# All twelve inner blocks of the last two batches in one run of groups, five of the pairs by Strassen's scheme

## The chip, the core and the metric

The kernel runs on one core of a Trainium2 chip. The metric is the device time of one execution in microseconds (us). The core has a matrix engine (TensorE, PE in the profile), three engines for elementwise work (VectorE as DVE, ScalarE as ACT, GpSimd as POOL) and a queue engine (SyncE, SP) from which nearly all DMAs are issued. Each engine runs its instructions in the order in which the program lists them. A difference of under 0.2% is about what a measurement of this kernel cannot tell from none.

## The reference, cut to what matters

```python
# q, k, v: (4 batches, 12 heads, 448, 64); weights are float64
scores = q @ k^T / 8, causal mask, softmax
x = softmax @ v                      # back to (4, 448, 768)
h = relu(x^T @ w_tok1) @ w_tok2      # mixes the 448 tokens through 256
u = x + h^T
out = u + relu(u @ w_ch1) @ w_ch2    # mixes the 768 channels through 1536
```

The channel mixer is the large part. Its 1536 inner channels are twelve **inner blocks** of 128. Each float32 operand is split into a high and a low part, so every product takes three matmuls: high by high, high by low, low by high.

## The kernel before, in words

**Attention** goes by pairs of heads, 24 pairs, six to a batch. `load_pair` and `prep` bring q and k in and transpose them. `heads` (L672) multiplies them (`qk`, line L695, fourteen small matmuls that the profile shows as 28 instructions). They use quarters of the array, 64 rows by 64 columns, and `QUARTERS` gives their order. The scores land in four PSUM banks, one for each entry of `ROUND`, and seven blocks follow: `low` on DVE (L712), `expo` on ACT (L724), then `guard`, `recip` and a normalisation each. Pairs 0 to 11 are turned by PE (`by_tensor`, L781). Pairs 12 to 23 are split into 16-bit halves, turned by DMA and merged (`by_dma`, L801). `values` (L882) multiplies by v, and `xturn` (L928) turns the result. The buffers `prob0` to `prob3` have two copies each. In `by_dma` a pair takes one copy for its probabilities and the other for the split halves, so the next pair's `qk` can begin only when the splits have read the first copy.

**The token mixer** (`tokens`, L974 and L1007) runs for each third of a batch and adds into `u`. `split_u` makes the high and low parts of `u`.

**The channel mixer** has two forms. `channels(stage)` (L1056) takes one quarter (three inner blocks) for the batches that `STAGES` names: 108 matmuls of 448 columns for a quarter and a batch. `group(number)` takes blocks for batches 2 and 3 together. A pair of blocks goes by Strassen's scheme: seven products of 9 matmuls (L1376) in place of 72, then the multiplication back (L1444), 72 matmuls. `mixtures` makes the sums T1 to T4 of the two batches that the scheme needs, `combined` the sums of the weights. `hidden` (L1304) applies the relu and makes high and low mid tiles, in the rings `gh` and `gl` of six. `add` (L1120) adds a result into `u`, and the last one of a batch and column block starts `store` or, at the very end, `finish` (L1457).

**The order of the work** is written by a planner. `Plan.job` records each step with its cost on the engines that may do it, its needs, the buffers it holds and a rank. `Plan.emit` (L137) steps through a modelled time: each free engine takes the ready step of lowest rank whose buffers are open. Attention of pair g has rank 2g. A plain stage has rank 27 plus 6 for each stage before it, so fills in on PE between the pairs. Evacuations and re-read weights have rank -5 or -6. In the first 75 us, when PE has nothing ready and the modelled busy share is low, `emit` puts in a filler matmul that computes nothing (`keep_warm`, L602). The real engines then follow this order, whatever the model got wrong.

Before the change `STAGES` is quarter 0 for batch 0; quarters 1, 2 and 3 for batches 0 and 1; quarter 0 for batches 1 and 2; quarter 3 for 2 and 3; quarter 0 for batch 3. `GROUPS` holds three pairs, blocks 3 to 8. The last stage runs after the groups.

Of the kernel before, what the change touches and what calls it, by code (L numbers as in the profile page):

```python
# [19 lines left out]

class Slot:


    def __init__(self, ring):
        self.ring = ring
        self.index = ring.uses
        self.left = 0
        self.tile = None
        ring.uses += 1

    def take(self):
        self.ring.taken.append(self)
# [16 lines left out]
class Bank:  # L49


    def __init__(self, plan, kind, share):
        self.plan, self.kind, self.share = plan, kind, share
        self.left = 0
        self.bank = None

# [4 lines left out]
    def take(self):  # L61
        p = self.plan
        self.bank = p.banks.pop(0)
        p.used[self.kind] = p.used.get(self.kind, 0) + 1
# [6 lines left out]
class Job:  # L71
    def __init__(self, order, costs, fn, rank, moved, lock=False):
        self.order, self.costs, self.fn, self.rank, self.moved, self.lock = order, costs, fn, rank, moved, lock
        self.waits = 0
        self.ready = 0.0
        self.after = []
        self.takes = []
        self.holds = []
        self.done = False
        self.engine = None  # L80


class Plan:
# [7 lines left out]
    WINDOW, KEEP, WARM = 3400.0, 0.65, 75000.0  # L91
    LAG = {"pe": 230.0, "act": 150.0, "dve": 150.0, "pool": 150.0, "sp": 100.0}
    OWN = {"pe": 0.0, "act": 100.0, "dve": 130.0, "pool": 100.0, "sp": 100.0}
# [28 lines left out]
    def job(self, costs, fn, needs=(), holds=(), rank=0.0, moved=0.0, lock=False):  # L122

        j = Job(len(self.jobs), costs, fn, rank, moved, lock)
        for n in needs:
            if n is not None:
                n.after.append(j)
                j.waits += 1
        for s in holds:
            if s.left == 0:  # L130
                j.takes.append(s)
            s.left += 1
            j.holds.append(s)
        self.jobs.append(j)
        return j

    def emit(self):  # L137
        now = 0.0
        free = dict.fromkeys(self.ENGINES, 0.0)
        port = {"dve": 0.0, "pool": 0.0}  # L140
        dma = 0.0

        def until(j, e, t):
# [3 lines left out]
            return t + j.costs[e]  # L147
# [17 lines left out]
        while left:  # L165
# [3 lines left out]
            for e in self.ENGINES:  # L169
# [4 lines left out]
                while ready[e]:  # L174
# [4 lines left out]
                    open_ = all(s.open() for s in j.takes) and self.fits(j)  # L179
# [29 lines left out]
                end = until(pick, e, now)  # L209
                if e == "pool" or (e == "dve" and pick.lock):  # L210
                    port[e] = end
                free[e] = end
                if e == "pe":
                    self.spans.append((now, end))
                if pick.moved:
                    dma = end = max(end + 650.0, dma) + pick.moved
                    end += 800.0
                heapq.heappush(events, (end, 0, pick.order, pick))
# [25 lines left out]
def kernel(  # L244
# [72 lines left out]
    def act_ps(n):  # L317
        return 160.0 + 0.833 * n

    def act_sb(n):  # L320
        return 200.0 + 0.833 * n

    def dve1(n):
        return 150.0 + 1.04 * n

    def dve2(n):
        return 150.0 + 0.55 * n

    def pool1(n):
        return 230.0 + 0.85 * n  # L330

    def pool2(n):
        return 270.0 + 2.1 * n

    def pe(*ns):
        return sum(max(109.0, 0.458 * n) for n in ns)

    def move(n):
        return n / 290.0
# [45 lines left out]
    def narrow(n, shape, source, f, rank, needs=(), raw=None):  # L385
# [31 lines left out]
        j = plan.job({"sp": 520.0}, load, holds=[raw], rank=rank, moved=move(shape[0] * n * 8))  # L417
        j = plan.job({"act": act_sb(n)}, size, [j, *needs], [raw, f], rank)
# [5 lines left out]
    def token_weights():  # L424
        work = [(w_tok1, w1hi, w1lo, c, 0, DT) for c in range(NCH)]
        work += [(w_tok2, w2hi, w2lo, c, o, S // 2) for c in range(NM) for o in (0, S // 2)]
        for n, (src, hi, lo, c, o, w) in enumerate(work):
# [10 lines left out]
            a = narrow(w, [P, 1, w], source, f, TRANK, raw=slot(("wh", "wl")[n % 2]))  # L438
# [17 lines left out]
    def channel_weights(stage, o):  # L456
# [5 lines left out]
        size = P * NT * P * 4  # L462
        if stage < NQT:
            def source():
# [12 lines left out]
                {"sp": 520.0},  # L477
                lambda e: nc.sync.dma_start(out=scratch[m], in_=flat(f.tile)),
                got, [f], rank, moved=move(size),
            )  # L480
        else:
            got = [plan.job(
                {"sp": 520.0},
# [3 lines left out]
                [saved[m]], [f], rank, moved=move(size),  # L487
            )]
        if stage == len(STAGES) - 1 and o < NF:

            wh, wl = slot("ws"), slot("wsl")
            p, q = homes_of(wh)

            def hi(e):
                wh.tile = home_of(wh, 0)
                copy(e, wh.tile, flat(f.tile))

            def lo(e):
                wl.tile = home_of(wh, 1)
                minus(e, wl.tile, flat(f.tile), wh.tile.bitcast(F32))  # L500

            w = NT * P
            a = plan.job({"act": act_sb(w), "pool": pool1(w)}, hi, got, [f, wh, p], rank)
            return wh, wl, a, plan.job(
                {"pool": pool2(w), "dve": dve1(w)}, lo, [a], [f, wh, wl] + list({p, q}), rank, lock=True
            )
        wh, wl = slot("wh"), slot("wl")
        a = plan.job(
            {"act": act_sb(NT * P), "pool": pool1(NT * P)},
            lambda e: copy(e, make(wh, [P, NT * P], F32R), flat(f.tile)), got, [f, wh], rank,  # L510
        )
        b = plan.job(
            {"pool": pool2(NT * P), "dve": dve1(NT * P)},
            lambda e: minus(e, make(wl, [P, NT * P], F32R), flat(f.tile), wh.tile.bitcast(F32)),
            [a], [f, wh, wl], rank, lock=True,
        )
        return wh, wl, a, b

    def reread(sources, saves, rank):
# [7 lines left out]
        return f, plan.job({"sp": 520.0}, load, saves, [f], rank, moved=move(P * NT * P * 4))  # L527
# [16 lines left out]
    def parts(f, got, rank):  # L544
# [3 lines left out]
            {"act": act_sb(NT * P), "pool": pool1(NT * P)},  # L548
            lambda e: copy(e, make(wh, [P, NT * P], F32R), flat(f.tile)), [got], [f, wh], rank,
# [15 lines left out]
    QUARTERS = ((0, 0, 6), (0, 1, 5), (1, 2, 4), (1, 3, 3), (0, 1, 1), (1, 3, 2), (1, 2, 0),  # L565
                (1, 1, 5), (1, 0, 6), (0, 3, 3), (0, 2, 4), (0, 3, 2), (0, 2, 0), (1, 1, 1))
# [59 lines left out]
    def load_pair(g):  # L626
        b, t = divmod(g, NT)
        for nm, src in (("k", k), ("q", q), ("v", v)):
# [26 lines left out]
            js = [plan.job({by: 520.0 * n}, fn, holds=[s], rank=2.0 * g + RL + (VL if nm == "v" else 0.0), moved=1274.0)]  # L655
# [16 lines left out]
    def heads(g):  # L672
# [16 lines left out]
        def qk(e):  # L689
            for r in range(len(ROUND)):  # L690
                bank(scores[r])
                kept(probs[r])
            for j, r, c in QUARTERS:
                lanes = LANES[1 - j if r in CROSS else j]
# [6 lines left out]
        holds = scores + probs + [ke, qe, stat]  # L701
        m = plan.job({"pe": 1900.0}, qk, ready + [last_qk[0]], holds, rank)
        last_qk[0] = m
        for r, cs in enumerate(ROUND):
            ps = scores[r]
            for c in cs:
# [22 lines left out]
                a = plan.job({"dve": 80.0 + dve1(wide(c))}, low, [m, start], [ps, probs[r], stat], rank)  # L729
                if start is None:  # L730
                    start = a
                exps.append(plan.job({"act": 480.0 + 0.833 * wide(c)}, expo, [a], [probs[r], stat], rank))
            for rg in RG:
                if r == rg[-1]:
# [13 lines left out]
                    rc = plan.job({"act": 230.0, "pool": 250.0, "dve": 170.0}, guard, exps, [stat], rank, lock=True)  # L748
                    rc = plan.job({"dve": 180.0}, recip, [rc], [stat], rank)
# [9 lines left out]
    def by_tensor(g, rcs, probs, stat, part, wide):  # L759
# [5 lines left out]
        for r, cs in enumerate(ROUND):  # L765
            norms = []
            for c in cs:
                def norm(e, c=c, r=r):
# [4 lines left out]
                    {"pool": pool1(w) + 90.0, "dve": dve2(w) + 60.0, "act": act_sb(w) + 95.0}, norm, [rcs[r]], [probs[r], stat], rank, lock=True  # L773
# [20 lines left out]
            a = plan.job({"pe": pe(0, 0, 0, 0)}, flip, norms + [prev, blank[f"prob{r}", probs[r].index % PB]], [ps, pt, probs[r]], rank)  # L794
# [6 lines left out]
    def by_dma(g, rcs, probs, stat, part, wide):  # L801
# [6 lines left out]
        for r, cs in enumerate(ROUND):  # L808
            both = halves[r]
            parts = [blank[f"prob{r}", probs[r].index % PB]]  # L810
            for c in cs:
                w = wide(c)

                def norm(e, c=c, r=r):
# [3 lines left out]
                    {"pool": pool1(w) + 90.0, "dve": dve2(w) + 60.0, "act": act_sb(w) + 95.0}, norm, [rcs[r]],  # L818
# [18 lines left out]
            a = plan.job({"sp": 1250.0}, turn, [a], [both, t16], rank, moved=1570.0)  # L837
# [15 lines left out]
            costs = {"act": 220.0 * n + 0.97 * 8 * P, "dve": 150.0 * n + 0.55 * 8 * P}  # L853
# [9 lines left out]
    def values(g):  # L863
# [10 lines left out]
        for part in ((0, 1), (2, 3)):  # L874
# [15 lines left out]
            cost = sum(52.0 + QC * STEPS[n][3] / 0.6 for n in part)  # L890
            prev = plan.job({"pe": cost}, pv, js + pdone + [prev], [ps, s, pt, u], rank)
# [14 lines left out]
        u_ready[b, t] = plan.job({"act": 200.0 + act_ps(S), "dve": 140.0 + dve1(S)}, evac, [prev] + first, [ps, u], rank)  # L906

    def xturn(g):
# [24 lines left out]
        a = plan.job({"pe": pe(0, 0, 0, 0)}, turn, [u_ready[b, t]], [ps, utile[b]], rank)  # L933
# [22 lines left out]
    u_split = {}  # L956
    us = {}

    def tokens(b, hf):
# [38 lines left out]
        for t in range(hf * NTH, (hf + 1) * NTH):  # L998
# [19 lines left out]
            u_split[b, t] = plan.job({"dve": dve1(S)}, plus, [a], [ps, utile[b]], WRANK)  # L1018
# [27 lines left out]
    def channels(stage):  # L1046
# [53 lines left out]
        for o in range(NF):  # L1100
            wh, wl, wa, wb = channel_weights(stage, NF + o)
            for i in range(2):
                for b in bs:
# [13 lines left out]

                    add(b, t, ps, prev, (stage, t) == (len(STAGES) - 1, NT - 1))

    def add(b, t, ps, prev, final=False):  # L1120
# [7 lines left out]
        if b == B - 1:  # L1128

            ready.append(unmixed[t])  # L1130
# [5 lines left out]
        if times + 1 == (NQT if b < 2 else 2 + len(GROUPS)):  # L1136
# [420 lines left out]
```

## Time and profile before

| | before |
|---|---|
| median of 3 runs | 565.9 us (565.84 to 566.09) |
| profiled execution, its own time | 566.33 us |
| its span, first to last instruction | 564.6 us |
| PE busy | 548.2 us (97%) |
| DVE, ACT, POOL busy | 395.0, 304.7, 223.1 us |
| granted TensorE clock | 1.0 throughout, 2.4 GHz |

A row of a group of instructions reads: line, engine, operation, written tile and read tiles, count, then busy time and mean duration of one, then idle time of the engine before them and what ended it. Matmuls are pipelined, so the duration of one is longer than the distance from one start to the next.

### The profile page before, as it was taken

To read this page: it belongs to the slowest core of one execution; us is meant where nothing else is said; L and a number is where in the kernel's file an instruction comes from. 1 tells how busy PE (TensorE), PEld (TensorE's weight loads), DVE (VectorE), ACT (ScalarE), POOL (GpSimd) and SP (SyncE) were. 2 spreads that over 40 slices of the span, in tenths; PEclk is the share of its full clock that TensorE was granted. 3 is DMA by queue.
4 is the path that set the end of the run, shared out by engine and by line. 5 is a ranking of instruction groups with operands and counts; after the bars stand their busy time and mean duration, and the time that the engine had idled before them with its cause. 6 is when DMAs were issued, how large, how long until landed. Compare 5 with 4: busy or idle time off the path is not lost.

```text
span 564.6 us, 10295 instructions
## 1 busy us (share of the span) xinstructions
PE 548.2 (97%) x3512; PEld 473.5 (84%) x3512; DVE 395.0 (70%) x925; ACT 304.7 (54%) x746; POOL 223.1 (40%) x320
## 2 busy tenths in 40 slices
PE   8789999999999999999999999999999999999996
PEld 4467888878888988988988988988999998999995
DVE  4575868588777677778867687566576668677835
ACT  3678888787687566776667754674143120111010
POOL 2465675535352321430353621353356546232001
PEclk9999999999999999999999999999999999999999
DMA  6777647576988689789996766766221030312525
GB/s 112 157 154 149 155 104 174 161 180 150 197 224 190 149 203 204 177 222 200 217 217 132 151 111 122 148 126 127 62 74 56 29 111 2 111 55 86 126 57 99
DMA packets 230340, 77.37 MB, mean 137 GB/s; under 512 B 206544, under 2 KB 219024, under 8 KB 230288
## 3 DMA queue, kind: packets, MB, share of 16 engines
q1 hardware_dynamic: 217056, 74.99, 58.6%
q10 hardware_dynamic: 13232, 1.72, 1.8%
q8 instruction: 28, 0.46, 0.3%
q14 instruction: 24, 0.20, 0.1%
HBM read 49.15 MB, written 14.94 MB: 114 GB/s over the span
## 4 chain that ended last, share of the span: by engine, by line
PE 90%; SPq 3%; ACT 3%; DMA 2%; DVE 1%; issue 0%; POOL 0%; DVEq 0%; ACTq 0%
PE ps L1056 48%; PE ps L1444 8%; PE ps L882 7%; PE ps L1376 6%; PE ps L1007 5%; PE ps L974 5%; PE ps L695 5%; PE ps L781 3%; SPq L635 2%; PE ps L928 2%; DMA wl<-in_moe_w_tok_dram 1%; ACT prob L724 1%; SPq L400 1%; ACT pt L343 0%; DMA kq<-in_q_dram 0%
## 5 line engine op out<-in xcount | busy, mean ns | idle before, releaser
L1124 DVE TENSOR_TENSOR u<-ps,u 128x448 f32<-128x448 f32 x107 | 66.3, 622 | 47.1 <-PE ps L1056 33.6
L724 ACT ACTIVATE prob<-prob,stat 128x448 f32<-128x448 f32 (+6 forms) x168 | 84.0, 504 | 26.1 <-DVE stat L712 25.9
L345 POOL TENSOR_SCALAR prob<-prob,stat 128x448 f32<-128x448 f32 (+6 forms) x125 | 69.9, 572 | 39.7 <-DVE stat L746 36.7
L1056 PE MATMUL ps<-gh,wh 128*128 128x448 f32 x216 | 80.6, 373 | 0.0
L1056 PE MATMUL ps<-gh,wl 128*128 128x448 f32 x216 | 79.0, 366 | 0.0
L1056 PE MATMUL ps<-gl,wh 128*128 128x448 f32 x216 | 79.0, 366 | 0.0
L1056 PE MATMUL ps<-uh,wh 128*128 128x448 f32 x198 | 75.0, 379 | 0.0
L1056 PE MATMUL ps<-uh,wl 128*128 128x448 f32 x198 | 72.5, 366 | 0.0
L1056 PE MATMUL ps<-ul,wh 128*128 128x448 f32 x198 | 72.4, 366 | 0.0
L345 POOL TENSOR_SCALAR wh<-wf 128x768 fp32r<-128x768 f32 x27 | 23.1, 854 | 113.4 <-PE ps L1056 65.1
L712 DVE CUSTOM_DVE_ANT_0 prob<-ps,mask 128x448 f32<-128x448 f32 (+6 forms) x168 | 62.3, 412 | 0.3 <-PE ps L695 0.3
L743 POOL TENSOR_SCALAR stat<-stat 128x3 f32<-128x3 f32 (+1 forms) x43 | 13.3, 309 | 96.5 <-ACT prob L724 95.0
L882 PE MATMUL ps<-pt,vraw 128*64 128x448 f32 (+3 forms) x384 | 46.8, 386 | 1.4 <-ACT pt L343 1.4
L882 PEld LDWEIGHTS ps<-pt,vraw 128*64 128x64 f32 x384 | 25.4, 136 | 25.0 <-issue 14.0
L349 ACT COPY pt<-pt 128x512 uint16<-128x512 uint16 (+1 forms) x46 | 36.8, 875 | 15.5 <-DMA pt<-prob 15.4
L1056 PEld LDWEIGHTS ps<-gh,wh 128*128 128x128 f32 x216 | 40.6, 188 | 3.7
L1056 PEld LDWEIGHTS ps<-gl,wh 128*128 128x128 f32 x216 | 40.6, 188 | 3.5 <-DVE gl L1092 0.3
L1056 PEld LDWEIGHTS ps<-gh,wl 128*128 128x128 f32 x216 | 40.5, 188 | 3.2
L695 PEld LDWEIGHTS ps<-kq,kq 64*64 64x64 f32 x672 | 36.0, 132 | 8.3 <-issue 4.2
L695 PE MATMUL ps<-kq,kq 64*64 64x448 f32 (+6 forms) x672 | 41.8, 383 | 0.0
L354 DVE TENSOR_TENSOR wl<-wf,wh 128x768 fp32r<-128x768 f32 x35 | 35.9, 1033 | 8.5 <-ACT wh L343 4.9
L1056 PEld LDWEIGHTS ps<-uh,wh 128*128 128x128 f32 x198 | 37.2, 188 | 3.7
(144 smaller groups left out, 1224.2 us busy)
## 6 DMA issues: line engine op xcount, KB each, us to landing
wraw<-in_moe_w_ch_dram SPq DMA_DIRECT2D x24, 768.0 KB, 5.3
wf<-scratch SPq DMA_DIRECT2D x30, 384.0 KB, 3.2
scratch<-wf SPq DMA_DIRECT2D x24, 384.0 KB, 5.8
vraw<-in_v_dram SPq DMA_DIRECT2D x48, 96.0 KB, 2.4
out_dram<-kq SPq DMA_DIRECT2D x68, 56.0 KB, 1.8
kq<-in_k_dram SPq DMA_DIRECT2D x60, 56.0 KB, 3.9
kq<-in_q_dram SPq DMA_DIRECT2D x56, 56.0 KB, 2.5
gh<-in_k_dram SPq DMA_DIRECT2D x36, 56.0 KB, 2.3
```

Source lines behind the costliest of these rows:

```text
L345: eng[e].tensor_scalar(dst, src, scale, 0.0, op0=ALU.mult, op1=ALU.add)
L349: nc.scalar.copy(out, in_)
L354: eng[e].tensor_tensor(dst, a, b, op=ALU.subtract)
L695: nc.tensor.matmul(scores[r].tile[lanes, WHERE[c]:WHERE[c] + wide(c)], lhsT=qe.tile[LANES[j], c * QC:(c + 1) * QC], rhs=ke.tile[LANES[j], ...
L712: nc.vector.tensor_tensor_reduce(out=part(c, r), in0=ps.tile[:, WHERE[c]:WHERE[c] + wide(c)], in1=mask[:, S - wide(c):], scale=-SCALE, sca ...
L724: nc.scalar.activation(part(c, r), part(c, r), AF.Exp, bias=stat.tile[:, 0, AT[c]:AT[c] + 1], scale=-1.0, accum_out=stat.tile[:, 1, AT[c]: ...
L882: nc.tensor.matmul(ps.tile[LANES[j], c * QC:(c + nq) * QC], lhsT=s.tile[:, kb, j], rhs=view[:, o:o + nq, j], start=(kb == 0), stop=(n == 3),)
L974: nc.tensor.matmul(ps.tile[:, :PART], lhsT=w[:, c, m * P:(m + 1) * P], rhs=x.tile[:, c, :], start=(n == 0), stop=(n == len(work) - 1),)
L1056: nc.tensor.matmul(ps.tile[:, :S], lhsT=x.tile[:, at_:at_ + P], rhs=y, start=(n == 0 and i == 0), stop=(n + 1 == w[2] and i == 2),)
L1124: eng[e].tensor_tensor(u, ps.tile[:, :S], u, op=ALU.add)
L1376: nc.tensor.matmul(ps.tile[:, :S], lhsT=l()[:, t * P:(t + 1) * P], rhs=r, start=(t == 0 and n == 0), stop=(t == half - 1 and n == 2),)
L1444: nc.tensor.matmul(ps.tile[:, :S], lhsT=l.tile[:, t * P:(t + 1) * P], rhs=r.tile, start=(n == 0), stop=(n == 3 * len(fs) - 1),)
```

## The change

It rewrites four things. The stages and groups are set anew, with five Strassen pairs for batches 2 and 3, block 11 alone first and block 10 joined to the last pair. A second home for mid tiles is used by every other group. `qk` becomes two steps, its matmuls in another order. The planner gets other costs, a model of the DMA rings, and a table `NUDGE` of about 130 rank shifts.

```diff
+NUDGE = {
+    "narrow.load": {3.5: -1, 16: -19, 22: -34, 23: 5, 25: -5, 26: -3, 27: -62},
+    "heads.low": {2: -26, 8: 3, 12: -4, 16: -0.2, 18: -16, 24: -9, 26: 2, 32: -1, 42: -41, 44: 11},
+    "group.product.do": {55.98: 6, 56.79: 21, 57.06: 6, 60.87: 9, 64.68: 38, 64.95: 46, 67.68: 14, 68.49: 15,
+        68.76: 37, 69.03: 17},
...
 class Plan:
-    WINDOW, KEEP, WARM = 3400.0, 0.65, 75000.0
-    LAG = {"pe": 230.0, "act": 150.0, "dve": 150.0, "pool": 150.0, "sp": 100.0}
+    LEAD, SWITCH, RING = 1400.0, 100.0, 128.0
+    SLACK, SETTLED = 1.1, 30000.0
+    WINDOW, KEEP, WARM = 3400.0, 0.7, 75000.0
+    LAG = {"pe": 200.0, "act": 145.0, "dve": 130.0, "pool": 80.0, "sp": 100.0}
...
+        name = fn.__qualname__.replace("<locals>.", "").partition(".")[2]
+        rank = rank + NUDGE.get(name, {}).get(round(rank, 3), 0.0)
...
-    STAGES = ((0, (0,)), (1, (0, 1)), (2, (0, 1)), (3, (0, 1)), (0, (1, 2)), (3, (2, 3)), (0, (3,)))
-    LAP = 0.0
-    GROUPS = ((3, 4), (5, 6), (7, 8))
+    STAGES = ((0, (0,)), (1, (0, 1)), (2, (0, 1)), (3, (0, 1)), (0, (1,)))
+    LAP = 0.1
+    FIRST_GROUP = 4.5
+    SPAN = (0.34, 0.68, 1.01)
+    GROUPS = ((11,), (0, 1), (2, 3), (4, 5), (6, 7), (8, 9, 10))
...
     def act_ps(n):
-        return 160.0 + 0.833 * n
+        return 65.0 + 0.833 * n
...
-    QUARTERS = ((0, 0, 6), (0, 1, 5), (1, 2, 4), (1, 3, 3), (0, 1, 1), (1, 3, 2), (1, 2, 0),
-                (1, 1, 5), (1, 0, 6), (0, 3, 3), (0, 2, 4), (0, 3, 2), (0, 2, 0), (1, 1, 1))
+    QUARTERS = ((0, 0, 6), (1, 0, 6), (0, 1, 5), (1, 1, 5), (0, 1, 1), (1, 1, 1),
+                (0, 3, 3), (1, 3, 3), (0, 2, 4), (1, 2, 4), (0, 3, 2), (1, 3, 2), (0, 2, 0), (1, 2, 0))
...
-        holds = scores + probs + [ke, qe, stat]
-        m = plan.job({"pe": 1900.0}, qk, ready + [last_qk[0]], holds, rank)
-        last_qk[0] = m
+        made = {}
+        for rg, cost in zip(RG, (930.0, 740.0)):
+            holds = [x for r in rg for x in (scores[r], probs[r])] + [ke, qe, stat]
+            m = plan.job({"pe": cost}, lambda e, rg=rg: qk(e, rg), ready + [last_qk[0]], holds, rank, tiled=True)
+            last_qk[0] = m
+            made.update(dict.fromkeys(rg, m))
...
-                a = plan.job({"dve": 80.0 + dve1(wide(c))}, low, [m, start], [ps, probs[r], stat], rank)
+                a = plan.job({"dve": 82.0 + 0.975 * wide(c)}, low, [m, start], [ps, probs[r], stat], rank)
...
-                exps.append(plan.job({"act": 480.0 + 0.833 * wide(c)}, expo, [a], [probs[r], stat], rank))
+                exps.append(plan.job({"act": 277.0 + 0.857 * wide(c)}, expo, [a], [probs[r], stat], rank))
...
-            at = 7.89 if stage == len(STAGES) - 1 else stage
-            return CRANK + CSTEP * (at + (0.5 if stage == len(STAGES) - 1 else 1.0) * (count - n) / total) - CLEAD
+            return CRANK + CSTEP * (stage + len(bs) * 0.5 * (count - n) / total) - CLEAD
...
-        if b == B - 1:
-            ready.append(unmixed[t])
+        if b >= B - 2:
+            ready += unmixed[b, t]
...
-            p1, i1, e1 = again(t)
-            p2, i2, e2 = again(t + half)
-            x1, j1, f1 = mix("T1", t, p1, at(u3, t), ALU.subtract, [i1] + n3, [e1, u3])
+            v = t + half
+            n2, m2, n3, m3 = u_whole[B - 2, t], u_whole[B - 2, v], u_whole[B - 1, t], u_whole[B - 1, v]
+            x1, j1, f1 = mix("T1", t, at(u2, t), at(u3, t), ALU.subtract, [n2, n3], [u2, u3])
...
+    def second_home():
+        if not second:
+            second.append(slot("u"))
+        x = second[0]
+        g = {n: [plan.slot("g2", 3), plan.slot("g3", 3), [x]] for n in ("11", "22", "12")}
...
+        g["21"] = [slot("h1h"), slot("h1l"), []]
+        return g
...
-            g = {n: (slot("gh"), slot("gl")) for n in names}
+            g = second_home() if number % 2 else {n: (slot("gh"), slot("gl"), []) for n in names}
...
-    for stage in range(len(STAGES) - 2):
+    mixtures()
+    for stage in range(len(STAGES)):
         channels(stage)
-    mixtures()
-    channels(len(STAGES) - 2)
-    for number in range(len(GROUPS)):
-        group(number, 6.0 + number * 0.63)
-    channels(len(STAGES) - 1)
+    at = FIRST_GROUP
+    for number, fs in enumerate(GROUPS):
+        group(number, at)
+        at += SPAN[len(fs) - 1]
```

`again`, which rebuilt batch 2's `u` from its parts, is gone, since no plain stage adds into batches 2 and 3 any more. Homes of the mixtures now include the token weights, dead by then. The wide copies of re-read weights may go to ACT alone, no longer to POOL. `add` finishes both batches at the last column block of the last group.

## Rows read from the trace of the kernel before

**Rows 1.** The page's first part: busy time, share of the span, instructions.

```profile
PE 548.2 (97%) x3512; PEld 473.5 (84%) x3512; DVE 395.0 (70%) x925; ACT 304.7 (54%) x746; POOL 223.1 (40%) x320
```

**Rows 2.** Busy time by stage: stretch, length, engines, clock, DMA share, GB/s.

```profile
7.00:60.00 53.00, 44.78 (x415) 32.60 (x418) 34.43 (x134) 39.61 (x129) 26.33 (x55) 1.00 0.72 144
60.00:127.00 67.00, 65.96 (x567) 56.40 (x561) 47.85 (x148) 55.99 (x169) 38.15 (x60) 1.00 0.62 158
...
163.00:372.00 209.00, 209.00 (x1337) 181.47 (x1336) 154.56 (x380) 137.80 (x302) 64.80 (x96) 1.00 0.80 175
372.00:403.60 31.60, 31.60 (x176) 28.41 (x174) 20.23 (x33) 14.67 (x31) 12.63 (x15) 1.00 0.56 116
...
453.00:536.00 83.00, 81.60 (x401) 74.82 (x400) 60.50 (x90) 11.83 (x19) 27.36 (x23) 1.00 0.29 83
536.00:560.00 24.00, 23.53 (x115) 21.15 (x114) 12.29 (x20) 2.49 (x4) 3.52 (x3) 1.00 0.40 74
560.00:565.00 5.00, 0.73 (x4) 0.37 (x4) 1.02 (x3) 0.00 (x0) 0.00 (x0) 1.00 0.47 94
```

**Rows 3.** PE's waits, 7 to 60 us (two) and 60 to 565 us (one).

```profile
PE ps L781 <- POOL prob L345: 3.6, 3, 1.5
PE ps L781 <- ACT prob L343: 1.9, 1, 1.9
...
PE ps L1444 <- DVE gl L1312: 1.4, 1, 1.4
```

**Rows 4.** Fillers: their group in 7 to 60 us; one run of twelve.

```profile
L602 PE MATMUL ps<-mask 128*128 128x512 bf16 x39 | 10.2, 380 | 0.0
...
8.76 2.76 PE L602 MATMUL ps<-mask 128*128 128x512 bf16 x12
```

**Rows 5.** The chain that ended last, 400 to 470 us: start, us, what.

```profile
403.76 49.45 PE ps L1056 x243
453.21 10.96 PE ps L1376 x54
...
465.46 2.06 DVE gl L1312
```

**Rows 6.** Line L1056 alone, up to the last token matmul and behind it.

```profile
0.00:403.60 403.60, 205.96 (x946) 173.54 (x946) 1.00 0.74 163
403.60:453.10 49.50, 49.50 (x243) 45.44 (x242) 1.00 0.18 50
```

**Rows 7.** The same chain: nine matmuls after whole-array work, and after a qk.

```profile
139.11 1.83 PE ps L1056 x9
...
195.39 1.66 PE ps L695 x14
197.06 2.04 PE ps L1056 x9
```

**Rows 8.** Timeline of pair 0: low on DVE, expo on ACT, blocks of 448 and 384.

```profile
9.64 0.59 DVE L712 CUSTOM_DVE_ANT_0 prob<-ps,mask 128x448 f32<-128x448 f32 x1
...
10.16 0.55 DVE L712 CUSTOM_DVE_ANT_0 prob<-ps,mask 128x384 f32<-128x384 f32 x1
...
10.28 0.67 ACT L724 ACTIVATE prob<-prob,stat 128x448 f32<-128x448 f32 x1 [6.20 <-DVE stat L712]
...
10.94 0.60 ACT L724 ACTIVATE prob<-prob,stat 128x384 f32<-128x384 f32 x1
```

**Rows 9.** Timeline of PE: first and last qk turned by DMA, last product with v.

```profile
126.99 1.74 PE L695 MATMUL ps<-kq,kq 64*64 64x448 f32 x28
...
363.03 1.74 PE L695 MATMUL ps<-kq,kq 64*64 64x448 f32 x28
...
388.79 1.95 PE L882 MATMUL ps<-pt,vraw 128*64 128x448 f32 x16
```

**Rows 10.** DVE by group, 403.6 to 453 us: adds, and differences of the mixtures.

```profile
L1124 DVE TENSOR_TENSOR u<-ps,u 128x448 f32<-128x448 f32 x14 | 8.7, 624 | 8.1 <-PE ps L1056 7.6
L1184 DVE TENSOR_TENSOR kq<-kq,kq 128x448 f32<-128x448 f32 x6 | 6.1, 1023 | 0.0
...
L1184 DVE TENSOR_TENSOR kq<-kq,u 128x448 f32<-128x448 f32 x3 | 1.9, 628 | 0.0
```

More of the change, by code (lines that the diff above doesn't have):

```diff
@@ L131, in job @@
                 j.takes.append(s)
+            elif s not in j.takes:
+                j.joins.append(s)
             s.left += 1
@@ L146, in until @@
                 t = max(t, port["dve" if e == "pool" else "pool"])
-            return t + j.costs[e]
+            return t + j.costs[e] * (self.SLACK if now >= self.SETTLED and e not in ("pe", "sp") else 1.0)
         ready = {e: [] for e in self.ENGINES}
@@ L178, in emit @@
                         continue
-                    open_ = all(s.open() for s in j.takes) and self.fits(j)
+                    open_ = all(s.got for s in j.joins) and all(s.open() for s in j.takes) and self.fits(j)
                     if open_ and len(j.costs) > 1:
@@ L486, in channel_weights @@
                 ),
-                [saved[m]], [f], rank, moved=move(size),
+                [saved[m]], [f], rank, moved=1200.0,
             )]
[L489 to L517, printed above, removed]
+        return parts(f, got, rank, stage >= NQT)
     def reread(sources, saves, rank):
@@ L835, in turn @@
                 nc.sync.dma_start_transpose(out=t16.tile[:, r], in_=both.tile.bitcast(U16))
-            a = plan.job({"sp": 1250.0}, turn, [a], [both, t16], rank, moved=1570.0)
+            a = plan.job({"sp": 1310.0}, turn, [a], [both, t16], rank, moved=1900.0, ring=73)
             def merge(e, r=r):
@@ L1116, in channels @@
                     )
[L1118 removed]
+                    add(b, t, ps, prev)
     def add(b, t, ps, prev, final=False):
@@ L1332, in place @@
             count += n
-            if len(fs) == 1:
-                return CRANK + CSTEP * (at + span * (count - n) / total) - CLEAD
             done = count - n
-            return CRANK + CSTEP * (at + (0.005 * done - LAP if done < 63 else 0.005 * done)) - CLEAD
+            return CRANK + CSTEP * (at + (0.005 * done - LAP if len(fs) > 1 and done < 63 else 0.005 * done)) - CLEAD
         gs = {b: [] for b in bs}
-        if len(fs) == 1:
-            wh, wl, wa, wb = parts(*up_block(fs[0], rank), rank)
+        split_block = parts if len(fs) == 1 else spared
@@ new lines, in group, with product, do, first @@
+        if len(fs) > 1:
+            ws = combined(*fs[:2], rank)
+            def product(wname, bname):
+                wh, wl, wd, wslots = ws[wname]
+                rows = [mixed[bname, t] for t in range(half)]
+                ps = share("w")
+                def do(e):
+                    bank(ps)
+                    for t in range(half):
+                        hi, lo = rows[t][0](), rows[t][1]()
+                        for n, (l, r) in enumerate(((wh, hi), (wh, lo), (wl, hi))):
+                            nc.tensor.matmul(
+                                ps.tile[:, :S], lhsT=l()[:, t * P:(t + 1) * P], rhs=r,
+                                start=(t == 0 and n == 0), stop=(t == half - 1 and n == 2),
+                            )
+                return ps, plan.job(
+                    {"pe": pe(*[S] * 9)}, do, wd + [j for r in rows for j in r[2]],
+                    [ps] + wslots + [z for r in rows for z in r[3]], place(9),
+                )
+            names = ("11", "22", "12", "21")
+            g = second_home() if number % 2 else {n: (slot("gh"), slot("gl"), []) for n in names}
+            def first(p):
+                f, (ps, j) = slot("kq"), p
+                def do(e):
+                    nc.scalar.copy(make(f, [P, S], F32), ps.tile[:, :S])
+                return f, plan.job({"act": act_ps(S)}, do, [j], [ps, f], WRANK - 1)
+            def plus(a, p, to=None, needs=()):
+                (src, ja), (ps, j) = a, p
+                f = to or slot("kq")
+                def do(e):
+                    if to is None:
+                        make(f, [P, S], F32)
+                    nc.vector.tensor_tensor(f.tile, src.tile, ps.tile[:, :S], op=ALU.add)
+                return f, plan.job(
+                    {"dve": dve1(S)}, do, [ja, j, *needs], [ps] + list({src, f}), WRANK - 1
+                )
+            def out_of(name, c):
+                f, j = c
+                return hidden(None, lambda: f.tile, *g[name][:2], [j], [f] + g[name][2])
+            p1 = product("A11", "B11")
+            c1 = first(p1)
+            p2 = product("A12", "B21")
+            p6 = product("S2", "T2")
+            p5 = product("S1", "T1")
+            p7 = product("S3", "T3")
+            p3 = product("S4", "B22")
+            p4 = product("A22", "T4")
+            u2 = plus(c1, p6)
+            r11 = out_of("11", plus(c1, p2, c1[0], [u2[1]]))
+            u4 = plus(u2, p5)
+            u3 = plus(u2, p7, u2[0], [u4[1]])
+            c22 = plus(u3, p5)
+            r22 = out_of("22", c22)
+            r12 = out_of("12", plus(u4, p3, u4[0]))
+            r21 = out_of("21", plus(u3, p4, u3[0], [c22[1]]))
+            gs[B - 1] = [r11, r21]
+            gs[B - 2] = [r12, r22]
@@ L1434, in group @@
-        downs = [parts(*down_block(f, rank), rank) for f in fs]
+        downs = [(split_block if n == 2 else parts)(*down_block(f, rank), rank) for n, f in enumerate(fs)]
         for t in range(NT):
```

304 lines of the change are left out of this document (164 added, 140 removed).

## The prediction

> **What bounds the kernel now.** I read the page's first part first: PE is busy for 97% of the span, and the next engine, DVE, for 70% [rows 1]. So time goes only with PE work, or with PE time that does no work. Busy time by stage shows where that second kind lies [rows 2]. From 60 us to the end PE is never idle for long: 1.0 us missing up to 127 us, nothing up to 453, 1.4 us in the groups, 0.5 behind them, 4.3 in the tail. In 7 to 60 us it is busy for 44.8 of 53 us, so 8.2 are idle. Part of what counts as busy there is filler: 39 filler matmuls, at 2.76 us for a run of twelve 0.23 each, 9.0 us [rows 4]. The head thus loses 17.2 us. PE's longest waits in it are for normalised tiles from POOL and ACT, 3.6 and 1.9 us [rows 3]: pairs of heads are not ready in time. The one wait of size later on is 1.4 us for a mid tile's low part [rows 3], at the border from products to the multiplication back. The chain that ended last shows the price of PE work: 243 matmuls in 49.45 us, 0.2035 us each [rows 5].
>
> **Part 1, fewer matmuls.** Plain quarters: before, 1+2+2+2+2+2+1 = 12 of 108 matmuls, 1296; three pairs at 63+72 add 405, in all 1701. After: 1+2+2+2+1 = 8 quarters, 864; block 11 alone 72; four pairs 540; the last group 63+36+108 = 207; in all 1683. Eighteen matmuls at 0.2035 us are **-3.7 us**, all on the path. Longer accumulations spare some adds on DVE, which is off the path; the two more pairs add sums and combined weights there, and DVE has 21 of 83 us spare in the group stage [rows 2].
>
> **Part 2, qk in two steps.** The same 28 instructions take 1.66 us in the chain; nine whole-array matmuls behind them take 2.04 us instead of 1.83 [rows 7]. So one visit to the quarter-array work costs 0.21 us, in and out together. Where other work comes between the halves there is a second visit. No row shows a half by itself: the ends are 0 (halves always adjacent) and 24 x 0.21 = 5.0 us. For pairs 0 to 11 I take them as adjacent. For the twelve turned by DMA the second half waits for the splits of its own two buffers, so other work comes between: 12 x 0.21 = **+2.5 us**.
> The Trainium skill, "TensorEngine Tiling (Array Packing)", Key Properties, says that a change of the tiling mode, not of the tile alone, drains the engine; it speaks against this part of the change. The 0.21 us in the row agrees with it.
>
> **Part 3, the second home.** Every other pair writes its mid tiles elsewhere, and `LAP` moves its products ahead of the last multiplications back, so PE has work while the low parts are made. The 1.4 us of [rows 3] go, between 0 and -1.4 for each border shown; I take **-1.4 us**. Next late would be the weights of the next pair, whose first matrix waits for two products of the pair before.
>
> **Part 4, the head.** Nothing is removed there, but pairs start differently. The planner booked 0.695 us for a `low` of 448 columns and 0.853 for its `expo`. The starts of the next blocks show 0.52 and 0.66 [rows 8]. The new formulas give 0.519 and 0.661. So the old plan held each pair for about 0.17 us a block too long on either engine, seven blocks a pair: 1.2 and 1.3, together 2.5 us, and put fillers and other work where the pair was in truth ready. The halved `qk` also lets `low` of the first two banks be planned before the last two are written, about 0.7 us of the 1.66. Six pairs begin in 7 to 60 us. The ends are 0, if DVE and ACT, busy for 34 and 40 of the 53 us, hand the waits on to each other, and -17.2, if all that is lost comes back. I take a third, **-6 us**, 1 us a pair: nearer to 0, because ACT is the busier engine there and its work stays. The changed costs and rank shifts can also lose here; that is inside the ends of the last rival.
>
> **Part 5, the cover behind attention.** This part can turn the sign. Before the last token matmul at 403.6 us PE ran 946 plain matmuls, and 243 more behind it [rows 6], while the sums for Strassen were made. After the change only 864 plain ones exist, plus about 30 of block 11 that need nothing of batch 3's last third. So PE has 52 fewer, 10.6 us, to put between the pairs, less the 2.5 us of part 2: its fill ends 8.1 us before the old place of that matmul, whatever the head gives to both. The twelve pairs turned by DMA start 21.5 us apart (126.99 to 363.03, eleven steps) and the last one's product with v starts at 388.79 [rows 9]. If the step shrinks by 0.7 us, 12 x 0.7 = 8.4 us, the tokens are in time. I expect more: 2.5 us of too-long booking per pair, and a first half that no longer waits for all four splits. PE is at 100% there and DVE at 154.6 of 209 us, ACT at 137.8 [rows 2], so there is room. Behind the last token matmul about two thirds of the sums, eight differences of 0.63 to 1.02 us, and twelve adds of 0.62 remain for DVE [rows 10]: some 7 + 7.5 us, with 3 us for low parts 17.5. PE's cover is the rest of block 11 and two products without sums, about 60 matmuls or 12.2 us. Five us are short unless batch 1's last quarter (22 us of PE) is still there, which it is when the pairs speed up. The ends are 0 and +13 (8 + 5); I take **+1 us**.
>
> DMAs: re-read weights stay at 30, loads, transposes and stores keep their count; SP's queue is moved past nothing new but the stores of batch 1. These must end before the second home, batch 1's old residual, comes free. Tail: two batches instead of one finish, but one inside the other's last 1.8 us of matmuls; 0, at most +0.5 us beside the 4.3.
>
> **Sum.** -3.7 + 2.5 - 1.4 - 6 + 1 = -7.6 us on the profiled execution's 566.3 us (span 564.6 and 1.7 around it): 558.7. That execution lies 0.4 above the median of 565.9, so **558.3 us**.
>
> **Rivals.**
> *The head comes back almost whole.* Thirteen of 17.2 us instead of 6: 551. For it: the fillers stand where the model, not the chip, said that nothing was ready. Against: ACT's 40 of 53 us.
> *PE runs dry behind attention* (slower). If the pairs' step does not shrink, the last token matmul stands 8 us behind the end of the fill, and the sums add 5: +13 in place of +1, 570.3. It decides where the step stays above 20.8 us. For it: PE was full there before only because stages of batches 2 and 3 could be put in. Against: booked costs that were too long, and DVE with a quarter of its time free.
> *Every half drains the array.* Part 2 at its upper end, +2.5 more, and the extra visits take the head's 6 us: 566.8, no change. The row gives the price of a visit, but not how often halves part.
> *The second home does nothing.* It is batch 1's residual buffer. If its stores come late, the first pair's low parts wait there and each of five borders keeps its 1.4 us: 7 us in place of 0, 565.3.
>
> **How the numbers follow.** Forecast 0.60, head 0.16, dry 0.13, drained array 0.07, no second home 0.04. The forecast's own range is 552 to 565 from the ends of parts 2 and 4. The low end, 549, takes in the first rival with some room. The upper end, 568, takes in the third and fourth and leaves most of the dry case out. A difference under 0.2% (1.1 us) is about what a measurement of this kernel can't tell from none. Faster by more: the forecast, the first rival and the odd part of the fourth, 0.79. Same: third and part of the fourth, 0.08. Slower: 0.13.
>
> **What would show it.** Right: 1683 matmuls on the three lines; fewer than 39 fillers and less than 8.2 us idle in 7 to 60 us; the pairs' step under 20.8 us; the last token matmul before 390 us; no PE wait of over 1 us at a border of groups. Wrong: a PE wait of several us for a mixture or a mid tile right behind the last token matmul, or a head as long as before.

## The result, and the profile after

The changed kernel takes **558.9 us** (median of 4, 557.7 to 560.3) against 566.0 for the one before in the same runs: ratio **0.987, 95% interval 0.985 to 0.990**. 558.3 was forecast. The profiled execution took 557.66 us with a span of 555.5 and a granted clock of 1.0.

The page's first part, and the stages of the kernel after (columns as in [rows 2]):

```profile
PE 547.3 (99%) x3492; PEld 462.8 (83%) x3492; DVE 413.9 (75%) x964; ACT 338.7 (61%) x820; POOL 159.9 (29%) x247
```

```profile
7.00:60.00 53.00, 50.69 (x470) 35.31 (x470) 38.79 (x154) 47.33 (x162) 26.94 (x59) 1.00 0.71 145
...
127.00:357.00 230.00, 230.00 (x1504) 195.76 (x1505) 177.64 (x420) 176.23 (x396) 75.19 (x99) 1.00 0.81 180
357.00:535.00 178.00, 178.00 (x863) 161.57 (x862) 134.21 (x212) 51.91 (x81) 16.58 (x13) 1.00 0.31 78
535.00:555.50 20.50, 16.72 (x85) 14.83 (x83) 10.64 (x19) 1.31 (x4) 0.00 (x0) 1.00 0.68 121
```

PE's missing time is now almost all in the head and the tail: 2.3 of 53 us idle in 7 to 60 us, where [rows 2] had 8.2; 0.7 from 60 to 127 us; nothing from 127 to 535 us; 3.8 in the tail. PE's waits in the head, and the only one behind it (in place of [rows 3]), then the fillers (in place of the first of [rows 4]):

```profile
PE ps L737 <- DVE kq L707: 1.4, 1, 1.4
PE ps L737 <- DVE stat L791: 0.9, 1, 0.9
...
PE ps L927 <- ACT pt L410: 0.5, 1, 0.5
```

```profile
L641 PE MATMUL ps<-mask 128*128 128x512 bf16 x34 | 9.2, 380 | 0.0
```

The 3.6 and 1.9 us waits for normalised tiles are gone, and so is the 1.4 us at the border of the groups. The plain channel line, up to the last token matmul and behind it ([rows 6]), and the timeline of PE at the first and last pair turned by DMA and the last product with v ([rows 9]):

```profile
0.00:357.00 357.00, 160.82 (x747) 137.80 (x747) 1.00 0.77 171
357.00:410.00 53.00, 24.32 (x117) 21.89 (x117) 1.00 0.59 127
```

```profile
113.46 1.75 PE L737 MATMUL ps<-kq,kq 64*64 64x448 f32 x28
...
310.10 1.09 PE L737 MATMUL ps<-kq,kq 64*64 64x448 f32 x12
311.13 1.95 PE L927 MATMUL ps<-pt,vraw 128*64 128x448 f32 x16
313.01 0.81 PE L737 MATMUL ps<-kq,kq 64*64 64x256 f32 x10
...
342.35 1.95 PE L927 MATMUL ps<-pt,vraw 128*64 128x448 f32 x16
```

The pairs' step is (310.10 - 113.46) / 11 = 17.9 us, from 21.5. The last token matmul stands 46 us earlier, and 117 plain matmuls still lie behind it. Of the channel lines there are 864 plain, 72 up-products of the two single blocks (11 and 10, 36 each), 315 products and 432 multiplications back: 1683, as forecast.

**Where the time went.** The trace was split at each PE start, the time up to the next start given to the instruction before it. The span fell by 9.1 us: idle time from 15.0 to 7.0 us (-8.0), fillers from 14.7 to 13.5 (-1.2), channel matmuls from 353.3 to 348.9 (-4.4), qk from 40.4 to 43.2 (+2.8), the turns of the probabilities by PE from 21.4 to 22.4 (+1.0), the rest +0.7. Idle and fillers together are called **PE's lost time** below: 29.7 us before, 20.5 after, of it in 7 to 60 us 17.2 and 10.1.

### The profile page after: what moved, and what is told of

Its sections match the earlier page's. It is cut to its first block, busy times and chain, and to the rows that moved or that the text cites. A ratio compares the mean times of both kernels' runs of the same rounds, so it can differ in the third digit from the quotient of the medians.

```text
span 555.5 us, 10290 instructions
## 1 busy us (share of the span) xinstructions
PE 547.3 (99%) x3492; PEld 462.8 (83%) x3492; DVE 413.9 (75%) x964; ACT 338.7 (61%) x820; POOL 159.9 (29%) x247
## 4 chain that ended last, share of the span: by engine, by line
PE 92%; ACT 3%; DMA 2%; SPq 1%; issue 1%; DVE 1%; POOL 0%; ACTq 0%; DVEq 0%; POOLq 0%
PE ps L1104 31%; PE ps L1523 16%; PE ps L1432 12%; PE ps L927 8%; PE ps L737 6%; PE ps L1021 5%; PE ps L1054 4%; PE ps L826 3%; PE ps L1503 3%; PE ps L641 2%; PE ps L973 2%; DMA wraw<-in_moe_w_ch_dram 1%; SPq L674 1%; ACT prob L769 1%; ACT pt L410 0%
## 5 line engine op out<-in xcount | busy, mean ns | idle before, releaser
L1104 PE MATMUL ps<-uh,wh 128*128 128x448 f32 x144 | 54.4, 378 | 0.0
L1104 PE MATMUL ps<-gh,wh 128*128 128x448 f32 x144 | 53.4, 370 | 0.0
L1104 PE MATMUL ps<-gl,wh 128*128 128x448 f32 x144 | 52.7, 366 | 0.0
L1104 PE MATMUL ps<-gh,wl 128*128 128x448 f32 x144 | 52.7, 366 | 0.0
L1104 PE MATMUL ps<-uh,wl 128*128 128x448 f32 x144 | 52.7, 366 | 0.0
L1104 PE MATMUL ps<-ul,wh 128*128 128x448 f32 x144 | 52.6, 366 | 0.0
L410 ACT ACTIVATE wh<-wf 128x768 fp32r<-128x768 f32 x21 | 17.3, 844 | 52.5 <-PE ps L1523 37.9
L737 PE MATMUL ps<-kq,kq 64*64 64x64 f32 (+6 forms) x672 | 45.8, 387 | 2.3 <-DVE kq L707 1.4
L769 ACT ACTIVATION_READ_ACCUMULATOR prob<-prob,stat 128x1 f32 x168 | 32.9, 196 | 0.0
L410 ACT ACTIVATE prob<-prob,stat 128x256 f32<-128x256 f32 (+5 forms) x65 | 27.7, 462 | 6.6 <-DVE stat L791 6.4
```

The costliest lines, as they stand in the source:

```text
L410: nc.scalar.activation(dst, src, AF.Copy, scale=scale)
L737: nc.tensor.matmul(scores[r].tile[lanes, WHERE[c]:WHERE[c] + wide(c)], lhsT=qe.tile[LANES[j], c * QC:(c + 1) * QC], rhs=ke.tile[LANES[j], ...
L769: nc.scalar.activation(part(c, r), part(c, r), AF.Exp, bias=stat.tile[:, 0, AT[c]:AT[c] + 1], scale=-1.0, accum_out=stat.tile[:, 1, AT[c]: ...
L1104: nc.tensor.matmul(ps.tile[:, :S], lhsT=x.tile[:, at_:at_ + P], rhs=y, start=(n == 0 and i == 0), stop=(n + 1 == w[2] and i == 2),)
```

## The experiments

All ratios are to the kernel before. PE's lost time and qk's time are counted as above, in one profiled execution of each kernel; a "visit" is a run of qk matmuls with nothing else between them.

| kernel | median us | ratio (95%) | lost time, all (7 to 60 us) | qk us, visits |
|---|---|---|---|---|
| before | 566.0 | 1 | 29.7 (17.2) | 40.4, 24 |
| after | 558.9 | 0.985 to 0.990 | 20.5 (10.1) | 43.2, 36 |
| e1 after again | 557.4 | 0.982 to 0.989 | 20.0 (10.3) | 43.2, 36 |
| e2 no shifts | 564.6 | 0.996 to 1.001 | 24.0 (11.0) | 44.1, 39 |
| e4 one home | 556.8 | 0.981 to 0.985 | 21.2 (10.4) | 43.2, 36 |
| e11 one home, no lap | 557.9 | 0.984 to 0.987 | 20.7 (10.3) | 43.3, 36 |
| e5 new plan, old structure | 569.2 | 1.004 to 1.007 | 25.1 (12.4) | 44.6, 38 |
| e8 first quarters joined | 580.2 | 1.024 to 1.027 | 37.1 (11.2) | 44.6, 38 |
| e5b one shift less | 560.7 | 0.989 to 0.992 | 20.7 (10.8) | 43.8, 38 |
| e9 same, qk whole | 566.8 | 1.001 to 1.004 | 30.3 (15.3) | 40.4, 24 |
| e10 same, halves for pairs 0 to 5 | 563.1 | 0.994 to 0.997 | 26.1 (8.9) | 42.1, 28 |
| e13 shifts of rank 24 up, and negative | 559.7 | 0.987 to 0.991 | 20.6 (10.0) | 43.5, 37 |
| e12 shifts of rank 0 to below 16 | 568.2 | 1.002 to 1.006 | 28.1 (12.9) | 43.3, 36 |
| e14 shifts of rank 24 up, qk whole | 571.7 | 1.007 to 1.011 | 32.0 (15.0) | 40.4, 24 |

### The changed kernel once more

No edit.

> The changed kernel once more, nothing edited. Median 557.5 to 560.5 us. In the trace on record its matmuls of 448 columns stand 206.7 ns apart in most of the group stage, 203 before. If that belongs to the program's order, it stands at the same places again; if it is chance of the execution, elsewhere or not at all.

Measured 557.4 us. The chain in the group stage shows what differed between the two profiled executions of one program; first the one after the change, then this one:

```profile
428.29 13.02 PE ps L1432 x63
441.31 14.68 PE ps L1523 x72
455.99 13.02 PE ps L1432 x63
```

```profile
428.26 12.77 PE ps L1432 x63
441.03 14.68 PE ps L1523 x72
455.71 12.77 PE ps L1432 x63
```

The same 63 products take 206.7 ns each in one execution and 202.7 in the other. So here the slower spacing is not the program's order. From 390 to 410 us, though, both executions run at 206.7, so the order is not ruled out everywhere. From 410 us on the mean is 205.9 ns against 203.1 over some 680 matmuls, about 1.9 us, which is as much as the 1.6 us between the two spans (555.5 and 553.9). What causes it stays open; differences of 2 us between single traces are to be read with it in mind.

### Without the rank shifts

```diff
-NUDGE = { ... }
+NUDGE = {}
```

> All rank shifts taken out, costs and structure kept. Theory A (the corrected costs bring the pairs of heads forward): head loses 10 to 12 us, 559 to 561 us. Rival B (the rank shifts do it): the head loses about 17 us again, 565 to 567 us, and the last token matmul ends behind 380 us instead of at 357.

Measured 564.6 us: nearly the whole gain is gone. But the head loses 11.0 us, not 17; the pairs' step is 17.2 us and the last token matmul stands at 353 us. So most of the regained head and the early tokens do not come from the shifts. Of the 6.8 us between the profiled spans (562.3 and 555.5), 3.5 are lost time (24.0 against 20.5), in waits such as these, in the head and behind it. The rest is PE's own work: qk +0.9, turns of the probabilities +0.9, of the results +1.0, plain matmuls +1.4, token matmuls +1.0, and -1.7 in the group stage, which is the spacing again:

```profile
PE ps L787 <- POOL prob L373: 2.7, 1, 2.7
...
PE ps L1484 <- DVE u L1356: 0.6, 1, 0.6
PE ps L1015 <- DVE h1l L995: 0.6, 1, 0.6
```

### One home for mid tiles, and then no lap either

```diff
-            g = second_home() if number % 2 else {n: (slot("gh"), slot("gl"), []) for n in names}
+            g = {n: (slot("gh"), slot("gl"), []) for n in names}
```

> The second home of mid tiles taken out: every group uses the same six buffers. Theory A: each of five borders has PE wait for a mid tile's low part as before, 1.4 us or more, 565 us (563 to 567). Rival (the next group's products hide it anyway or the order adapts): within 1 us of the changed kernel, 558 to 560.

Measured 556.8 us: not slower. No PE wait stands at a border of groups. For the second kernel `LAP = 0.0` was added.

> The changed kernel with one home (which ran at 556.8 us) and LAP at 0, so that the products of a group no longer stand ahead of the last multiplications back of the group before. Theory D (the lap, not the second home, took the border wait away): PE waits 1.4 to 2 us for a low part at three to five borders, 561 to 565 us. Rival (the planner fills the border in any case): 556 to 558, no such wait.

Measured 557.9 us. PE's waits from 60 us to the end of that kernel, all of them:

```profile
PE ps L1523 <- DVE gl L1395: 0.5, 1, 0.5
PE ps L927 <- ACT pt L410: 0.2, 1, 0.2
```

Of the 1.4 us that [rows 3] show, 0.5 come back. A product reads mixtures and combined weights, no mid tile, and with one home the plan still lays products of the next pair ahead of a pair's multiplication back, or among it: two or three (18 or 27 matmuls) in e4, one or two in e11. The second home buys nothing that can be measured, and the lap half a us of waiting.

### The new plan on the old structure

The stages, groups and mixtures of before, with the new planner, the divided `qk` and its new order, without the shifts.

> The stages, groups and mixtures of before, with the new planner costs, its DMA model and the two-step qk, no rank shifts. Theory A: head 17.2 to 10 us lost, pairs 12 to 23 start 18 us apart instead of 21.5, qk 2.9 us dearer, no fewer matmuls, border wait 1.4 us stays: 566.3 - 7 + 3 = 562 (561 to 563.5). Rival B (rank shifts or the new stages do it): 567 to 569.

Measured 569.2 us: **slower**, about what the rival said. The head loses 12.4 us instead of 17.2 and the pairs' step is 18.5 us, yet the whole gains nothing. Its wait at the border, and its plain line behind the last token matmul:

```profile
PE ps L1480 <- DVE gl L1348: 1.4, 1, 1.4
```

```profile
376.70:480.00 103.30, 79.76 (x390) 73.30 (x390) 1.00 0.25 64
```

Attention ends 27 us earlier, but 498 plain matmuls (390 of them up to 480 us) then wait behind it: PE was full there before, so an earlier end is worth nothing. qk and the turns cost 4.3 and 2.1 us more, which is above the 4.6 us of lost time that it saves, and for one stretch the clock was at half (columns as in [rows 2]):

```profile
40.00:53.50 13.50, 10.08 (x95) 6.98 (x94) 8.67 (x37) 10.45 (x32) 4.47 (x10) 1.00 0.62 112
53.50:56.90 3.40, 3.18 (x15) 2.13 (x20) 0.40 (x2) 1.28 (x3) 0.69 (x2) 0.50 1.02 252
```

The granted clock fell to 1.2 GHz after 13.5 us in which PE was idle for 3.4.

From this and e2: planner and halves +3.3 us, the new stages and groups -4.6, the shifts -7.2; the three make -8.5 against e1. Taken in another order the shares could differ, and within the planner the costs, the DMA model and the new order of qk's matmuls were not tried apart.

### Both first quarters in one stage

Batch 1's quarter 0 no longer stands alone.

```diff
-    STAGES = ((0, (0,)), (1, (0, 1)), (2, (0, 1)), (3, (0, 1)), (0, (1,)))
+    STAGES = ((0, (0, 1)), (1, (0, 1)), (2, (0, 1)), (3, (0, 1)))
```

> Batch 1's first quarter back in one stage with batch 0's, so no quarter stands alone before the groups. Theory A (117 plain matmuls behind the last token matmul are more cover than needed): the quarter runs earlier, cover left is block 11 and two products, 12 us against 17 of sums on DVE: PE waits 2 to 5 us there, 559 to 563 us. Rival (the attention ends early enough that the cover stays, whichever quarter it is): no wait, within 1.5 us of the changed kernel.

Measured 580.2 us, 21 us slower than the changed kernel, far more than any theory had. PE's waits behind the last token matmul, then the chain (start, us, what), then three stretches (columns as in [rows 2]):

```profile
PE ps L1432 <- ACT u L410: 6.2, 1, 6.2
PE ps L1523 <- ACT u L1391: 5.0, 1, 5.0
PE ps L1523 <- DVE u L1395: 1.7, 1, 1.7
```

```profile
406.16 0.65 DVE h1l L1573
406.82 0.32 SPq L1577
...
408.23 1.83 DMA out_dram<-h1l
...
410.86 0.85 ACT u L410
411.75 13.54 PE ps L1432 x54
...
429.31 1.69 DVE kq L1462 x3
...
433.12 1.42 DVE u L1395
434.58 8.65 PE ps L1523 x29
```

```profile
400.00:409.40 9.40, 5.58 (x28) 4.83 (x26) 7.32 (x13) 0.00 (x0) 0.42 (x1) 1.00 0.23 39
409.40:416.20 6.80, 4.45 (x11) 3.61 (x12) 4.10 (x7) 1.61 (x3) 1.36 (x1) 0.50 0.59 100
...
429.80:440.10 10.30, 6.25 (x16) 5.20 (x17) 7.79 (x12) 3.61 (x6) 2.84 (x2) 0.50 0.10 35
```

For the first wait, 6.2 us, the chain goes from the store of an output, its DMA, into a combined weight (L410) and then into the first product. The combined weights lie in batch 0's old residual buffer, the second home in batch 1's, and both come free only when these batches' last stage is stored. With batch 1's lone quarter last, batch 0's buffer is free some 22 us of PE work earlier. **What that quarter covers first is a buffer's release, not the differences of the mixtures on DVE.** The second wait, 5.0 and 1.7 us, has another chain: from 425 to 434.6 us it runs through DVE, by the sums of the products (L1462) and the low parts of the mid tiles (L1395). Whether it would come without the first wait is not shown. The waits of some 13 us come with two stretches at half clock, 17 us long, the first behind 9.4 us in which PE was busy for 5.6; one more, of 3.4 us, stands in the head at 54.4 us.

### The halves of qk

The first three kernels here are the changed one less one shift (`"xturn.turn": {11: 22}`), since with it the planner finds no order of the work once qk is undivided, be it for all pairs or from pair 6 on. First that alone, as the control:

> The changed kernel less one rank shift (the transposes at rank 11), which the next two leave out too because the plan with undivided qk cannot be laid with it. Both theories: 557 to 561 us, some reordering of the head.

560.7 us, 1.8 slower than the changed kernel. Then qk in one piece, its matmuls in the new order:

```diff
-        for rg, cost in zip(RG, (930.0, 740.0)):
+        for rg, cost in (((0, 1, 2, 3), 1670.0),):
```

> The changed kernel less one rank shift (that control ran at 560.7 us, its span 558.8), with qk of a pair in one step again, in the new order of its matmuls. Theory A (a separated half costs a visit and nothing of it is needed once PE is full): qk at 40.4 us of PE instead of 43.8; the head gives some back because low starts later; 557.5 to 560 us. Rival C (the halves bring the pairs forward): pairs 12 to 23 again 20 us or more apart instead of 16.9, the last token matmul behind 380 us, 563 us or more.

566.8 us, 6 slower, though qk itself takes 3.4 us less. PE's lost time grows by 9.6 us; 9.6 - 3.4 = 6.2 is the difference. In 7 to 60 us there are 50 fillers, against 29 in the control. The time is as Rival C had it, but not by its mechanism: the pairs' step is 17.6 us and the last token matmul stands at 362 us, where it asked for 20 us or more and 380. So the early tokens do not come from the halves. Halves for pairs 0 to 5 alone (`if g < 6`):

> As that control, but qk halved for pairs 0 to 5 alone and undivided from pair 6 on. Theory A: keeps the head, spares the visits behind it: 557 to 559.5 us, the best of the three. Rival C: pairs 12 to 23 over 20 us apart, over 562 us.

563.1 us: the head loses even less (8.9 us), but 60 to 127 us lose 5.1 where the control loses nothing. So the halves pay in the later pairs turned by PE as well.

That the shifts had been fitted to the halves could still explain e9. So both were made again with other shifts, first with the halves, keeping those of rank 24 and more, or negative; then with qk whole, keeping those of rank 24 and more alone. The second thus lacks six shifts of negative rank that the first has (in `xturn.lo`, `parts`, `add.plus`, `store.turn`, `store.send` and `group.plus.do`), so the two differ in more than the halves:

> The changed kernel with only those of its shifts whose rank is 24 or more, or negative: the work from pair 12 on and the channel steps. Theory A: it gives back the later stretch, some 3 us, 561 to 562.5 us, with a head like the one without shifts (11 us lost in 7 to 60 us, idle and fillers). Rival B, one fitted set: 564 us or more.

> The kernel with the later shifts alone, and qk undivided. Theory C, that the halves pay by themselves since low of the first two banks starts early: slower than the divided kernel by 4 to 7 us although some 3 us of quarter-array time go away, with more fillers and a longer pairs' step. Rival D, that the undivided kernel before was 6 us slower only because the early shifts had been fitted to the halves: same as the divided one within 1 us, or up to 3 us faster.

559.7 with halves and 571.7 without: 12 us, which is not the price of the halves alone. Lost time grows by 11.4 us and qk falls by 3.1. Of the lost time 5.0 us lie in the head, where no shift of rank 0 to below 24 is left in either kernel and only one of the six acts (the low part of the first pair's turn). There the rival finds no support. Some 5 us more lie behind 127 us: 3.4 are two waits at 419 to 423 us for mid tiles in the second home. There e12 and e2, which lack the same six shifts but have the halves, wait 1.6 and 0.6 us. And the clock was at half for 3.4 and 6.8 us, where e13 had it at 1.0. That part can't be put down to the halves, and whether the shifts were fitted to the halves stays open for what lies behind the head. The pairs' step is the same, 17.3 and 17.2 us. Fillers in 7 to 60 us, with halves and without:

```profile
L630 PE MATMUL ps<-mask 128*128 128x512 bf16 x26 | 6.8, 379 | 0.1
```

```profile
L625 PE MATMUL ps<-mask 128*128 128x512 bf16 x50 | 13.9, 379 | 0.3
```

The timeline of PE shows it for the same pair, pair 5, with halves and then without:

```profile
42.94 1.09 PE L726 MATMUL ps<-kq,kq 64*64 64x448 f32 x12
...
44.99 0.97 PE L726 MATMUL ps<-kq,kq 64*64 64x256 f32 x16
```

```profile
44.71 0.81 PE L625 MATMUL ps<-mask 128*128 128x512 bf16 x3
45.35 0.60 PE L810 MATMUL ps<-across_ident,prob 128*128 128x128 f32 x4
45.79 0.59 PE L625 MATMUL ps<-mask 128*128 128x512 bf16 x2
46.22 0.60 PE L810 MATMUL ps<-ident,prob 128*128 128x128 f32 x4
46.66 0.38 PE L625 MATMUL ps<-mask 128*128 128x512 bf16 x1
46.97 1.75 PE L721 MATMUL ps<-kq,kq 64*64 64x448 f32 x28
```

By the diff's `holds`, an undivided qk needs four PSUM banks and four probability buffers open at once; here it stands behind the last turns, with fillers between them. Divided, its first half asks for two of each, and stands 4 us earlier.

### The first shifts alone

Only shifts of rank 0 to below 16. Those of rank 16 to below 24 stand neither here nor in e13.

> The changed kernel with only those of its shifts whose rank is from 0 to below 16, which is the work of the first eight pairs; the later ones and the negative ranks are dropped. Theory A, that each part of the table pays where it stands: the kernel without any shifts loses 1.8 us more than the changed one in 30 to 60 us, 2.3 in 60 to 127, 2.8 up to the last token matmul. So this part gives back some 2 to 4 of the 7 us: 560.5 to 562.5 us, with the stretch up to 60 us like the changed kernel's and the later ones like those without shifts. Rival B, that the table is one fitted set, of which a part is worth nothing: 564 us or more.

568.2 us: 3.6 slower than without any, with 43 fillers in the head instead of 30. Rival B had the time (564 or more), but not that a part can do harm: the first shifts alone cost 3.6 us, and those of e13 alone give 4.9 of the 7.2 us. The whole table gives the rest, with the ranks from 16 to below 24 in it, which were not tried alone. The table is no sum of its parts as far as these two show; why the early shifts by themselves make the head worse stays open.

## Why the prediction held, step by step

The total was right within 0.6 us, and several terms were not right for the reason given, so that it came this close is in part luck. Two figures of the working do not follow from their sources: the ends of parts 2 and 4 give 545 to 567 us, not 552 to 565, and DVE has 22.5 us spare in the group stage by [rows 2], not 21. Neither moves the sum.

**Part 1, -3.7.** Right: 1683 matmuls. The channel matmuls took 4.4 us less (6.3 in e1, by its shorter spacing).

**Part 2, +2.5.** The size is right (+2.8 us, 12 extra visits at 0.24 us), the place is not. The prediction took pairs 0 to 11 as adjacent and the twelve turned by DMA as parted. The trace shows nine of the first and three of the second parted. As a gain it gave the halves no more than 0.7 us a pair, in part 4. With the shifts of the change, they gain 9.6 us of PE's lost time for the 3.4 that they take (e9 against its control), some 6 us net.

**Part 3, -1.4.** The wait went, but not by the second home (e4) and by the lap for at most 0.5 us (e11). The fourth rival, that the home does nothing, had its first half right; the five waits that it priced at 7 us do not come: in e4 the plan has two or three products of the next pair ahead of each multiplication back that has a pair behind it.

**Part 4, -6.** The head gave back 7.1 us (17.2 to 10.1). The step that failed is the split of the cause: the too-long costs were given 2.5 us a pair and the halves 0.7. With the new planner and whole qk the head still loses 15.3 and 15.0 us (e9, e14), against 10.8 and 10.0 with halves (e5b, e13). So the halves give some 5 us, and the costs with the rest of the planner and the shifts some 2.

**Part 5, +1.** The tokens came at 357 us, far before the 390 that it asked for, so nothing ran dry. The rival stood on the step: it decides above 20.8 us, and 17.9 was measured. Of the two reasons given for a shorter step, the first half of qk is not one, since the step is 17.6 and 17.2 us with whole qk (e9, e14); it leaves the planner, whose costs were not tried apart. Where the cover is missing (e8), PE waits first for a buffer, 6.2 us, then for sums of products and low parts, 6.7 us, not for the mixtures, and 21 us are lost instead of 13.

**What no term had: the shifts.** They were put down as a possible loss inside the last rival's ends. They are worth 7.2 us on this structure, spread over the kernel. Against that stands what the prediction gave to the plan by itself: costs and halves alone lose 3.3 us on the old structure (e5). Errors of both signs met in the sum.

The Trainium skill, "TensorEngine Tiling (Array Packing)", Key Properties, says that a change of the tiling mode drains the engine. The 0.24 us for an extra visit agrees that there is a cost. The whole came out the other way: e5b makes 14 visits more than e9 and loses 9.6 us less to fillers and idle time.

## What to carry to other kernels

Dividing a step that needs several buffers at once can be worth more than the entry cost of its second half (here 9.6 us for 3.4): look in the timeline for what stands ahead of the undivided step (fillers, waits), and count that beside the price of a visit. A shorter critical chain is worth nothing where the engine was full beside it; it pays only when the work that is left behind it goes too. Before work is taken from behind a chain, find which buffer's release it covers, in the chain of waits as well as in the list of homes. And two kernels that are to differ in one thing are to be compared line by line first: e13 and e14 differ in seven.

## What was not expected of the hardware

The same 63 matmuls of 448 columns ran at 202.7 ns each in one execution and 206.7 in another of the same program, both at a granted clock of 1.0. Both spacings also occur within one execution (e1: 206.7 from 390 to 410 us, 202.7 from 428 us).

The granted clock fell to 0.5 for 3.4 to 10 us at a time in four kernels whose PE had just been idle for a part of a stretch: it was busy for 10.1 of 13.5 us in e5, 5.6 of 9.4 in e8, 17.5 of 19.1 in e10, and 11.4 of 13.8 and 9.6 of 11.3 in e14. In e9 PE waited for 2.3 us at a stretch (at 341 us) and the clock stayed at 1.0, so the length of a wait alone does not tell it apart. In the changed kernel's profiled execution it did not fall before the end.
